# Six feed-forward chunks as seven block products per two chunks, weight sums on GpSimd, attention in two sets of buffers

## The chip, the cores and the metric

The kernel runs on one core of one Trainium2 chip. The metric is the device time of one execution in microseconds (us). Three executions of the kernel before took 1272.78, 1272.90 and 1273.23 us; the median is 1272.9 us. Engines are named as the profile names them: PE (matrix products; PEld is its weight load), DVE (vector), ACT (scalar), POOL (GpSimd), SP (which issues most of the DMAs).

## The reference

Linear attention with random features feeds a gated feed-forward layer. Attention has 8 batches of 8 heads with 576 tokens and 64 columns, so 4608 tokens of 512 columns enter the feed-forward layer, whose hidden width is 1536.

```python
def phi(x):
    proj = einsum('bhsd,df->bhsf', x, w_phi)
    proj = proj - max(abs(proj), axis=-1, keepdims=True)
    return concatenate([exp(proj), exp(-proj)], axis=-1)
q_p, k_p = phi(q), phi(k)
kv = einsum('bhsf,bhsd->bhfd', k_p, v);  z = sum(k_p, axis=2)
num = einsum('bhsf,bhfd->bhsd', q_p, kv)
den = einsum('bhsf,bhf->bhs', q_p, z)[..., None] + 1e-06
x = (num / den).transpose(0, 2, 1, 3).reshape(4608, 512)
g = x @ w_gate;  silu = g * (1.0 / (1.0 + exp(-g)));  val = x @ w_val
return silu * val @ w_out
```

## The kernel before

**Precision.** Most products are built from fp32r operands: a number is split into a high part (ACT rounds it) and a low part (DVE subtracts the high part), and a product is three matmuls: high by high, high by low, low by high. In the trace such an fp32r matmul is one record; a matmul of plain fp32 operands is two records.

**Feed-forward.** The tokens are cut into 12 chunks of 384 (`CH`), the hidden width into 12 strips of 128 (index `f`). `first(c, f, ...)` (L686) computes gate and value of chunk c in strip f: for each of two outputs (banks gv0 and gv1) four blocks of 128 input columns, three matmuls each, so 24 matmuls of 128x384. ACT then takes the tanh (L716) and DVE multiplies twice (L718, L721); `parts` splits the hidden strip into hh (ACT, L741) and hl (DVE, L742). `second(c, f, ...)` (L747) is nine matmuls of 128x512 into the three banks o0 to o2. `put_off` issues the second layer of strip f behind the first layer of strip f+1, so that PE has work while ACT and DVE make the hidden strip. The high parts of the weights stay in SBUF; the low parts are read from DRAM (`low_parts`, L669), anew for each chunk.

**Attention.** `attention(i, rank)` (L341) does one pair of heads, 32 pairs in all, four to a batch. The first eight pairs (`EARLY_PAIRS`) use plain fp32 products and two sets of buffers; the other 24 use one set, and split K, Q, the exponentials of Q (qh and ql, L577 to L583) and the sums kv (kvh and kvl, L456 and L460). The numerators (L593) are products of 128x288: four per pair, each of six fp32r matmuls in a late pair and of two fp32 matmuls in an early one. Behind them DVE divides (L616 to L620), and the result is split into xh and xl (L632, L634), which the first layer reads.

**The order.** Nothing is ordered by hand around the change. Every step is added to a `Plan` with an engine, a cost, the steps that it follows and a rank. `Plan.run` (L88) plays these through and writes out each engine's instructions in a fixed order: the ready step of lowest rank goes first. Attention has its pair number as rank on all engines, feed-forward steps on ACT, DVE and SP have rank -1 (`FIRST`), and feed-forward products on PE have ranks over 1000, so that they fill what attention leaves. Where PE has nothing ready in the plan, it gets products with zeros (L835 to L839), until the last strip of the first chunk.

## Time and profile before

| | |
|---|---|
| three executions | 1272.78, 1272.90, 1273.23 us |
| span of the profiled execution | 1273.1 us |
| instructions | 19796 |
| mean granted PE clock | 0.996 |
| HBM | 131 GB/s over the span |

The span runs from the first to the last instruction of one core; it lies 0.2 us over the median of the three times, so span and time are used alike below. Busy time is the union of an engine's instructions. PE records of neighbouring matmuls overlap (an fp32r matmul of 128x384 is shown with some 335 ns), so what a matmul costs PE is read from the distance of the starts, or from the chain of waits, where a row merges neighbours.

### The profile page before, as it was taken

What the parts mean: (1) busy time and instruction counts of PE and PEld (TensorE: products, weight loads), DVE (VectorE), ACT (ScalarE), POOL (GpSimd) and SP (SyncE); (2) the same over time, 40 slices, a digit from 0 to 9 for tenths busy, and PEclk for the clock granted to TensorE, in tenths of its full rate; (3) what the DMA queues carried; (4) which work ended last, traced back from release to release, by engine and by line L of the source; (5) the groups of instructions that cost most, each with busy time, mean ns of one, the idle gap of its engine ahead of it and who ended that gap; (6) DMA issues with size and microseconds to landing.
All of it is one profiled execution on the core that took longest, in us unless ns stands there. A gap on an engine that the chain in (4) does not pass through costs nothing.

```text
span 1273.1 us, 19796 instructions
## 1 busy us (share of the span) xinstructions
PE 1262.2 (99%) x7427; PEld 1189.9 (93%) x7427; DVE 876.4 (69%) x1674; ACT 651.5 (51%) x1383; POOL 1.3 (0%) x13
## 2 busy tenths in 40 slices
PE   9999999999999999999999999999999999999998
PEld 8887999999889999999999999999999999999998
DVE  6998999998887778762788888822488886222222
ACT  5787433336676666632765666611466665121211
POOL 0000000000000000000000000000000000000000
PEclk8999999999999999999999999999999999999999
DMA  4543455555564344444433444354444342444443
GB/s 120 144 119 102 140 174 175 174 165 167 159 204 123 112 117 113 148 123 127 129 104 113 129 124 120 105 161 129 125 120 119 105 132 84 124 149 125 149 126 106
DMA packets 112111, 168.15 MB, mean 132 GB/s; under 512 B 52752, under 2 KB 59408, under 8 KB 112016
## 3 DMA queue, kind: packets, MB, share of 16 engines
q1 hardware_dynamic: 111552, 166.64, 44.1%
q8 instruction: 58, 0.95, 0.3%
q14 instruction: 37, 0.30, 0.1%
q10 hardware_dynamic: 464, 0.26, 0.1%
HBM read 143.26 MB, written 23.59 MB: 131 GB/s over the span
## 4 chain that ended last, share of the span: by engine, by line
PE 92%; DVE 4%; DMA 1%; ACT 1%; SPq 1%; issue 0%; DVEq 0%; ACTq 0%
PE gv L282 46%; PE o L282 25%; PE work L282 12%; PE kv L435 8%; PE kv L428 1%; DMA out_dram<-osb 0%; PE o L502 0%; DVE km L410 0%; DVE kp L415 0%; DMA shared<-in_wg_dram 0%; DMA shared<-in_wo_dram 0%; DVE qy L491 0%; DMA wbd<-in_w_phi_dram 0%; DVE km L486 0%; ACT den L609 0%
## 5 line engine op out<-in xcount | busy, mean ns | idle before, releaser
L282 PE MATMUL gv<-xh,w_hi 128*128 128x384 f32 x1152 | 388.6, 337 | 0.8 <-DVE th L718 0.8
L282 PE MATMUL gv<-xh,w_lo 128*128 128x384 f32 x1152 | 386.9, 336 | 0.0
L282 PE MATMUL gv<-xl,w_hi 128*128 128x384 f32 x1152 | 386.1, 335 | 0.0
L282 PEld LDWEIGHTS gv<-xh,w_hi 128*128 128x128 f32 x1152 | 216.4, 188 | 5.7 <-DVE th L718 1.1
L282 PEld LDWEIGHTS gv<-xl,w_hi 128*128 128x128 f32 x1152 | 216.5, 188 | 4.6
L282 PEld LDWEIGHTS gv<-xh,w_lo 128*128 128x128 f32 x1152 | 216.1, 188 | 0.0
L716 ACT ACTIVATE th<-gv 128x384 f32<-128x384 f32 x144 | 70.9, 492 | 263.9 <-PE gv L282 263.1
L718 DVE SCALAR_TENSOR_TENSOR th<-th,gv 128x384 f32<-128x384 f32 x144 | 79.2, 550 | 149.6 <-ACT th L716 147.7
L282 PE MATMUL o<-w_hi,hl 128*128 128x512 f32 x432 | 171.5, 397 | 0.2 <-DVE hl L742 0.2
L282 PE MATMUL o<-w_hi,hh 128*128 128x512 f32 x432 | 170.9, 396 | 0.3 <-ACT osb L782 0.3
L282 PE MATMUL o<-w_lo,hh 128*128 128x512 f32 x432 | 170.3, 394 | 0.0
L741 ACT CAST hh<-th 128x384 fp32r<-128x384 f32 x144 | 73.6, 511 | 164.3 <-DVE th L721 148.1
L721 DVE TENSOR_TENSOR th<-th,gv 128x384 f32<-128x384 f32 x144 | 79.4, 552 | 71.1 <-PE gv L282 68.7
L435 PEld LDWEIGHTS kv<-vf,kp 128*128 128x128 f32 x1024 | 123.2, 194 | 3.1 <-ACT kp L419 1.3
L435 PE MATMUL kv<-vf,kp 128*128 128x66 f32 x1024 | 123.2, 274 | 1.3 <-ACT kp L419 1.0
L742 DVE TENSOR_TENSOR hl<-th,hh 128x384 fp32r<-128x384 f32 x144 | 79.5, 552 | 32.8 <-ACT hh L741 32.1
L282 PEld LDWEIGHTS o<-w_hi,hl 128*128 128x128 f32 x432 | 81.4, 188 | 19.4 <-DVE hl L742 0.6
L282 PEld LDWEIGHTS o<-w_hi,hh 128*128 128x128 f32 x432 | 81.7, 189 | 12.7 <-ACT osb L782 0.8
L282 PEld LDWEIGHTS o<-w_lo,hh 128*128 128x128 f32 x432 | 81.4, 188 | 12.2
L616 DVE STREAM_TRANSPOSE qe<-den 128x576 f32<-128x576 f32 x32 | 24.9, 778 | 92.0 <-ACT den L609 92.0
L607 ACT COPY num<-work 64x288 f32<-64x288 f32 x102 | 40.2, 394 | 51.2 <-PE work L282 49.8
L282 PE MATMUL work<-qh,kvh 128*128 128x288 f32 x192 | 60.8, 317 | 0.3 <-DVE kp L415 0.3
(124 smaller groups left out, 1871.1 us busy)
## 6 DMA issues: line engine op xcount, KB each, us to landing
w_lo<-wlo_dram SPq DMA_DIRECT2D x108, 512.0 KB, 3.6
w_lo<-wlo_dram SPq DMA_DIRECT2D x132, 256.0 KB, 3.0
wlo_dram<-w_lo SPq DMA_DIRECT2D x36, 256.0 KB, 2.3
out_dram<-osb SPq DMA_DIRECT2D x35, 256.0 KB, 3.3
kin<-in_kT_dram SPq DMA_DIRECT2D x32, 256.0 KB, 2.9
vf<-in_v_dram SPq DMA_DIRECT2D x64, 128.0 KB, 2.7
qin<-in_qT_dram SPq DMA_DIRECT2D x24, 288.0 KB, 2.9
shared<-in_wg_dram SPq DMA_DIRECT2D x12, 512.0 KB, 3.6
```

Source lines behind the costliest of these rows:

```text
L282: nc.tensor.matmul(o, l, r, start=a, stop=z)
L428: nc.tensor.matmul(ps_kv[:, 2 * k * D2:2 * (k + 1) * D2], room[:, 0, k], vf[j][:, 4].rearrange("p h d -> p (h d)"), start=False, stop=k == 1)
L435: nc.tensor.matmul(o, room[:, 2 * (t - t0) + h, k], vf[j][:, t, h], start=t + h + k == 0, stop=False)
L607: copied.append(add("ACT", act(SH), lambda key=key, ra=ra, c=c: nc.scalar.copy(num[ra, c], work[plan.bank[key]][ra, :SH]), [nu, free], rank))
L616: t0 = add("DVE", dve(S), lambda: vec.transpose(turned, den), [*copied, *done[0], *done[1]], rank)
L716: s1 = add("ACT", act(CH), lambda: nc.scalar.activation(t_, ps_gv[0][:, :CH], AF.Tanh, scale=0.5), [ends[0], th_free[j]], FIRST)
L718: s2 = add("DVE", dve(CH), lambda: nc.vector.scalar_tensor_tensor(out=t_, in0=t_, scalar=1.0, in1=ps_gv[0][:, :CH], op0=ALU.add, op1=ALU.m ...
L721: s3 = add("DVE", dve(CH), lambda: nc.vector.tensor_tensor(out=t_, in0=t_, in1=ps_gv[1][:, :CH], op=ALU.mult), [s2, ends[1]], FIRST)
L741: s4 = add("ACT", act(CH), lambda: nc.scalar.copy(hh[b], th[j]), [made, hid_free[b]], FIRST)
L742: s5 = add("DVE", dve(CH), lambda: nc.vector.tensor_tensor(out=hl[b], in0=th[j], in1=hh[b], op=ALU.subtract), [s4], FIRST)
```

## The change

The last six chunks are no longer done one by one. They are taken two at a time (chunks 6 and 7, 8 and 9, 10 and 11), and for each strip f the eight block products of {gate, value} by {two halves of the input columns} by {two chunks} are replaced by seven products of sums of blocks (Winograd's form of Strassen's product). One block product is six matmuls of 128x384.

- `operands(c)` loads the four blocks of x of two chunks from DRAM, makes sums and differences of them (DVE, 128x768), and splits the seven operands (ACT and DVE, 128x768), once for two chunks.
- `weights(m)` makes the four sums of weight blocks of a strip on POOL: four additions of high and low part (`whole`) and four subtractions (`combine`), each 128x256; ACT then rounds the 128x1024 result (`g2`) and DVE subtracts for the low part (`g3`). One buffer, b_full, holds the sums, two sets hold the results.
- `pair(c, base, ready)` issues the seven products of a strip (p1, p2, p6, p7, p5, p4, p3, called p by their names in the code) into banks gv0 and gv1, with three copies of gv0 by ACT (`copy`) and three additions by DVE (`joined`) that build the four results, and between them, one by one as `part(n)`, the six parts of the second layer of the strip before, for both chunks, into six banks.
- The low weights of the first layer are read once for two chunks.

All buffers of attention and of the pair stage become views of four big tiles (`m1`, `m2`, `a1`, `a2`), each of which is allocated up to three times in turn. So the names in the order and the trace are these tiles from now on. Attention has two sets of buffers throughout. The numerators of the 24 late pairs are plain fp32 products; the splits of the exponentials and of kv are gone, and so is the split of K of pair 8. All attention is finished before the pair stage begins; results of tokens of chunks 6 to 11 are stored to DRAM (x_dram) and not split there.

Core of the diff:

```diff
+PAIRS = 6
+LOW_SETS = 3
+ROOM = {"m1": 6912, "m2": 5140, "a1": 2432, "a2": 2048}
+URGENT = -0.8
+T_SETS = 2
+LOW2_SETS = 4
...
-    kin, qin = [sb("kin", [P, SK])] * 2, [sb("qin", [P, SK])] * 2
-    vf = [sb("vf", [P, 5, 2, D2])] * 2
-    kp = sb("kp", [P, 2, 2, 2, NF], F32, 2)
-    kvs = sb("kvs", [P, 4 * P], F32, 2)
-    qx, qe = sb("qx", [P, 2, S], F32, 2), sb("qe", [P, 2, S], F32, 2)
-    num, den = sb("num", [P, S]), sb("den", [P, S])
...
+    qx, qe = ([view("m1", [2, S]) for _ in range(2)] for _ in range(2))
+    kp = [view("m1", [2, 2, 2, NF]) for _ in range(2)]
+    kvs = [view("m2", [4 * P]) for _ in range(2)]
+    qy = [view("m2", [4, NF]) for _ in range(2)]
+    kin, qin = [view("m2", [SK])] * 2, [view("m2", [SK])] * 2
+    vf = [view("m2", [5, 2, D2])] * 2
+    num, den = view("m2", [S]), view("m2", [S])
...
-        split = not early
-        j = i % 2 if early else 1
+        plain = i <= EARLY_PAIRS
+        j = i % 2
+        one = 0 if early else j
...
-        if split:
-            for ones in range(2):
-                kvc.append(add("DVE", dve(4 * D), lambda ones=ones: vec.tensor_tensor(
-                    out=cut(kv_low(), ones), in0=sums(ones), in1=cut(kv_high(), ones), op=ALU.subtract),
...
-        done = [[f1], [f1]]
-        if split:
-            done = [[], []]
-            for h in range(2):
-                for k in range(2):
-                    part = (qe, qx)[k][j]
-                    def rounded(k=k, h=h, part=part):
-                        take_over()
-                        nc.scalar.copy(qh[k][:, h], part[:, h])
-                    g0 = add("ACT", act(S), rounded, [(f0, f1)[k][h], last.get(("nu", i - 1)), *weights_done], rank)
-                    done[h] += [g0, add("DVE", dve(S), lambda k=k, h=h, part=part: vec.tensor_tensor(
-                        out=ql[k][:, h], in0=part[:, h], in1=qh[k][:, h], op=ALU.subtract), [g0, f1[h]], rank)]
...
+        done = [[f1], [f1]] if early else [[f1[h]] for h in range(2)]
...
-                        if split:
-                            kvh, kvl = kv_high(), kv_low()
-                            terms += [(kvh[:, n], qh[k][:, h, c]), (kvl[:, n], qh[k][:, h, c]), (kvh[:, n], ql[k][:, h, c])]
-                        else:
-                            terms.append((kvs[j][:, n], (qe, qx)[k][j][:, h, c]))
+                        terms.append((kvs[j][:, n], (qe, qx)[k][j][:, h, c]))
...
-                nu = add("PE", 6 * pe(SH) if split else 2 * pe32(SH), numerators, [*done[h], *kvc, nu], rank, take=key)
-                free = last.get(("num", i - 1))
+                nu = add("PE", 2 * pe32(SH), numerators, [*done[h], *kvc, nu], rank, take=key)
...
+        held = [(start, width) for c, at, start, width in cuts if c >= PAIRS]
+        if held:
+            start, width = held[0][0], sum(w for _, w in held)
+            token = b * S + start - PAIRS * CH
+            x_stored[b, pr] = add("SP", P * width * 4, lambda start=start, width=width, token=token: nc.sync.dma_start(
+                x_dram[pr, :, token:token + width], num[:, start:start + width]), [t3], rank)
+            last["num", i].append(x_stored[b, pr])
...
+    attend(PAIRS * CH)
+    spread = []
+    for c in range(EARLY, PAIRS):
+        if c == PAIRS - 1:
+            attend(NCH * CH)
...
+        def whole():
+            for n in range(4):
+                gp.tensor_tensor(out=full()[:, block(n)], in0=hi[:, block(n)], in1=get(low)[:, block(n)], op=ALU.add)
+        def combine():
+            x = full()
+            for o, l, r in ((0, 2, 0), (2, 3, 2), (3, 3, 0), (1, 1, 3)):
+                gp.tensor_tensor(out=x[:, block(o)], in0=x[:, block(l)], in1=x[:, block(r)], op=ALU.subtract)
+        g0 = add("POOL", 4 * pool2(2 * P), whole, [low_at[m], *b_free], NEXT)
+        g1 = add("POOL", 4 * pool2(2 * P), combine, [g0], NEXT)
+        g2 = add("ACT", act(8 * P), lambda: nc.scalar.copy(th_(), full()), [g1, *t_free[u]], NEXT)
+        g3 = add("DVE", dve(8 * P), lambda: nc.vector.tensor_tensor(out=t(), in0=full(), in1=th_(), op=ALU.subtract), [g2], NEXT)
+        b_free[:] = [g3]
+        lo_free[k].append(g0)
+        t_free[u] = []
+        t_at[m] = [g2, g3]
...
+        d1 = combine(s1, a21, a22, ALU.add, [got[2], got[3], *temp_free[4]])
+        d2 = combine(s2, s1, a11, ALU.subtract, [d1, got[0], *temp_free[5]])
+        d3 = combine(a21, a11, a21, ALU.subtract, [d1, got[0]])
+        l0 = split(0, a11, [got[0]])
+        l1 = split(1, a12, [got[1]])
+        l2 = split(2, s2, [d2])
+        l3 = split(3, a21, [d3])
+        l4 = split(4, s1, [d1])
+        l5 = split(5, a22, [got[3]])
+        d4 = combine(a12, a12, s2, ALU.subtract, [l1, d2])
+        l6 = split(6, a12, [d4])
...
+            def mult(j, o, begin, final, after, m=m, low=low, hi=hi, tl=tl, t_hi=t_hi):
+                if j in (0, 1, 6):
+                    at = block((0, 1, None, None, None, None, 3)[j])
+                    w = lambda: (hi[:, at], get(low)[:, at])
+                    made = [low_at[m]]
+                    free = lo_free[m % LOW_SETS]
+                else:
+                    at = block((3, 2, 0, 1)[j - 2])
+                    w = lambda: (t_hi()[:, at], tl()[:, at])
+                    made = t_at[m]
+                    free = t_free[m % T_SETS]
...
+                    w_hi, w_lo = (x.rearrange("p (k f) -> p k f", k=2) for x in w())
+                    a_hi, a_lo = get(op_hi[j]), get(op_lo[j])
+                    terms = [x for k in range(2) for x in (
+                        (w_hi[:, k], a_hi[:, k]), (w_hi[:, k], a_lo[:, k]), (w_lo[:, k], a_hi[:, k]))]
+                    for i, (l, r) in enumerate(terms):
+                        nc.tensor.matmul(o[:, :CH], l, r, start=begin and i == 0, stop=i == len(terms) - 1, skip_group_check=True)
...
+            def copy(n, after):
+                return add("ACT", act(CH), lambda: act_.copy(snap[n](), bank_b[:, :CH]), [after, *snap_free[n]], FIRST)
+            def joined(n, after):
+                return add("DVE", dve(CH), lambda: vec.tensor_tensor(
+                    out=snap[n](), in0=bank_c[:, :CH], in1=snap[n](), op=ALU.add), after, FIRST)
...
+            p1 = mult(0, bank_b, True, False, b_read)
+            y1 = copy(0, p1)
+            p2 = mult(1, bank_c, True, True, c_read)
+            g1 = joined(0, [p2, y1])
+            ja, ga = gate(snap[0], [g1])
+            p6 = mult(2, bank_b, False, False, [y1])
+            y2 = copy(1, p6)
+            part(0)
+            part(1)
+            p7 = mult(3, bank_b, False, False, [y2])
+            y3 = copy(2, p7)
+            part(2)
+            p5 = mult(4, bank_c, True, False, [g1])
+            v2 = joined(2, [p5, y3])
+            p4 = mult(5, bank_b, False, True, [y3])
+            jb, gb = gate(bank_b[:, :CH], [p4])
+            part(3)
+            p3 = mult(6, bank_c, False, True, [v2])
+            v1 = joined(1, [p3, y2])
+            part(4)
+            part(5)
+            b_read[:], c_read[:] = [gb], [v1]
+            hb = valued(jb, 2, [gb, v2])
+            side_b = parts(jb, hb)
+            ha = valued(ja, 1, [ga, v1])
+            side_a = parts(ja, ha)
+            snap_free[:] = [[ga], [ha], [hb]]
+            waiting.append((c, f, side_a, side_b, low2(m), (outs, last_half) if final else None))
...
+    weights(0)
+    weights(1)
+    for n in range((NCH - PAIRS) // 2):
+        pair(PAIRS + 2 * n, NFT * n, operands(PAIRS + 2 * n))
+    at, g, ha_, hb_, lo2, tail = waiting.pop()
+    second(at + 1, g, hb_, lo2, range(NT), NT, tail)
+    second(at, g, ha_, lo2, range(NT), 0, tail)
```

What moves on the engines is seen in their order at three places. The first is PE, in the first layer of a late chunk: of before, the end of the value sum of chunk 10, where xh_98 and xl_101 are the chunk's parts, w_hi_76 and w_lo_94 the strip's weights, and the rows that follow are the second layer of the strip before.

```order
L282 MATMUL gv_144<-xh_98,w_hi_76 128x384
L282 MATMUL gv_144<-xl_101,w_hi_76 128x384
L282 MATMUL gv_144<-xh_98,w_lo_94 128x384
L282 MATMUL o_140<-w_hi_87,hh_130 128x512
L282 MATMUL o_140<-w_lo_95,hh_130 128x512
L282 MATMUL o_140<-w_hi_87,hl_132 128x512
```

Now, in the last pair of chunks: a part of the second layer (work_133), then the product p5 (into gv_130) and the start of p4 (into gv_129), whose weights are the sums in m_2_6847.

```order
L312 MATMUL work_133<-w_hi_84,hh_118 128x512
L312 MATMUL work_133<-m_2_6847,hh_118 128x512
L312 MATMUL work_133<-w_hi_84,hl_120 128x512
L1006 MATMUL gv_130<-a_2_6959,m_2_6847 128x384 x6
L1006 MATMUL gv_129<-xh_100,m_2_6847 128x384
L1006 MATMUL gv_129<-xl_103,m_2_6847 128x384
L1006 MATMUL gv_129<-xh_100,m_2_6847 128x384 x2
```

Of matmuls of 128x384 with operands the whole program has 3456 before and 3240 now; those of 128x512 stay at 1296. A strip of two chunks is now 42 and 18 of them in turn, with parts of the second layer between the products, instead of 48 and 18.

The second place is PE, in the numerators of a late pair. Before, with the exponentials' parts qh and ql and the sums' parts kvh and kvl:

```order
L282 MATMUL work0_146<-qh0_2562,kvh_1212 128x288
L282 MATMUL work0_146<-qh0_2562,kvl_1229 128x288
L282 MATMUL work0_146<-ql0_2563,kvh_1212 128x288
L282 MATMUL work0_146<-qh1_2564,kvh_1212 128x288
L282 MATMUL work0_146<-qh1_2564,kvl_1229 128x288
L282 MATMUL work0_146<-ql1_2565,kvh_1212 128x288
```

Now, for the last pair, where m1_0_104 holds the exponentials and m2_0_105 the sums, with a piece of a first layer between two numerators:

```order
L312 MATMUL work1_133<-m1_0_104,m2_0_105 128x288 x2
L312 MATMUL work0_132<-m1_0_104,m2_0_105 128x288 x2
L312 MATMUL gv1_130<-xh2_100,w1_hi7_77 128x384
L312 MATMUL gv1_130<-xl2_103,w1_hi7_77 128x384
L312 MATMUL gv1_130<-xh2_100,w1_lo1_95 128x384
```

Each of the 96 late numerators is two fp32 matmuls where it was six fp32r ones. The last of them stands 145 rows ahead of the first block product.

The third place is ACT in a late strip. Before, it does a tanh and a cast per strip:

```order
L716 ACTIVATE th_127<-gv_143 128x384
L741 CAST hh_131<-th_127 128x384
L716 ACTIVATE th_128<-gv_143 128x384
L741 CAST hh_130<-th_128 128x384
L716 ACTIVATE th_129<-gv_143 128x384
```

Now one strip of two chunks, where L1014 copies the bank gv0, L1024 is the tanh of the one and the other chunk, L922 the cast of the weight sums that POOL made (it waits for POOL), and L765 the casts of the two hidden strips:

```order
L1014 COPY m_2_6850<-gv_129 128x384 [waits PE_49,Activation_49]
L1024 ACTIVATE th_114<-m_2_6850 128x384 [waits DVE_49]
L1014 COPY a_2_6891<-gv_129 128x384 [waits PE_49] x2
L1024 ACTIVATE th_115<-gv_129 128x384 [waits PE_49]
L922 CAST m_2_6847<-a_2_6891 128x1024 [waits Pool_49]
L765 CAST hh_118<-th_115 128x384 [waits DVE_49]
```

ACT executes in this order; behind the cast that waits for POOL stand the casts of the hidden strips and the first copy of the next strip.

More of the change, by code (lines that the diff above doesn't have):

```diff
@@ L59 @@
 class Plan:
-    LAG = {"PE": 220, "ACT": 90, "DVE": 90, "SP": 2000}
+    LAG = {"PE": 220, "ACT": 90, "DVE": 90, "POOL": 200, "SP": 2000}
     BYTES = 250.0
@@ L135, in start @@
                 n += 1
-                heapq.heappush(events, (freed if t.eng == e and e in ("ACT", "DVE", "PE") else done, n, "dep", t))
+                heapq.heappush(events, (freed if t.eng == e and e in ("ACT", "DVE", "PE", "POOL") else done, n, "dep", t))
             if s.give is not None:
@@ new lines, in attention, with clear @@
+        use = lambda name: [last.get((name, i - 2)), last.get((name + "'", i - 2))]
+        if i == EARLY_PAIRS + 1:
+            def clear():
+                nc.gpsimd.memset(vf[1]()[:, :, :, D:], 1.0)
+                for h in range(2):
+                    nc.gpsimd.memset(vf[1]()[h * D:(h + 1) * D, 4, 1 - h], 0.0)
+                    nc.gpsimd.memset(kin[1]()[h * D:(h + 1) * D, 4 * P + (1 - h) * D:4 * P + (2 - h) * D], 0.0)
+            last["vf", i - 2] = last["kin", i - 2] = last["qin", i - 2] = add("POOL", 1000, clear, weights_done, rank)
@@ L363, in attention @@
         else:
-            q_in = [add("SP", P * S * 4, lambda: nc.sync.dma_start(qin[j][:, :S], qT[b, pr]), [last.get(("qin", i - 1))], rank)]
+            q_in = [add("SP", P * S * 4, lambda: nc.sync.dma_start(get(qin[one])[:, :S], qT[b, pr]), before("qin"), rank)]
         n = 4 * P * P
@@ L399, in project @@
                     acc = o[:, :NF] if tail else o[:, (t - t0) * 256:(t - t0 + 1) * 256]
-                    if early:
-                        matmuls([(acc, kin[j][:, c], wst if tail else wbd, True, True)])
+                    if plain:
+                        matmuls([(acc, get(kin[one])[:, c], wst if tail else wbd, True, True)])
                     else:
-                        khi, klo = (k_parts()[:, n, c] for n in range(2))
+                        khi, klo = (ks()[:, n, c] for n in range(2))
                         w_hi, w_lo = (wst_hi, wst_lo) if tail else (wbd_hi, wbd_lo)
@@ L440, in attention @@
         last["khi", i] = kproj
-        if early:
+        if plain:
             last["kin", i] = kproj
@@ L621, in attention @@
         last["qe", i] = t1
-        last["qx", i], last["qx'", i] = (done[0][-1], done[1][-1]) if split else (nu, None)
+        last["qx", i], last["qx'", i] = nu, None
         odd = b % 2
@@ L792, in favor_attention_moe @@
+            u = osb[n % len(osb)] if tail is None else tail[0][base + t]
+            cp = add("ACT", act(DM), lambda o=o, u=u: nc.scalar.activation(get(u), o, AF.Copy, scale=0.5),
+                     [done, out_done.get(n - len(osb)) if tail is None else None], FIRST)
+            stored[base + t] = [cp]
+            out_done[n] = add("SP", P * DM * 4, lambda u=u, rows=rows: nc.sync.dma_start(rows(), get(u)), [cp], FIRST)
     made = [0]
@@ new lines, in favor_attention_moe, with weights @@
+    b_free = list(ended)
+    t_free = [list(ended) for _ in range(T_SETS)]
+    for k in range(NT, 2 * NT):
+        stored[k] = list(ended)
+    low_at, t_at = {}, {}
+    def weights(m):
+        f = m % NFT
+        gp = nc.gpsimd
+        k, u = m % LOW_SETS, m % T_SETS
+        low, hi, t, th_, full = lo_bufs[k], flat(w1_hi[f]), t_low[u], t_high[u], b_full
+        after, lo_free[k] = lo_free[k], []
+        low_at[m] = add("SP", P * 8 * P * 4, lambda: nc.sync.dma_start(get(low).bitcast(F32), wlo_dram[f, :, :2 * DM]),
+                        [lo_stored[f, 0], lo_stored[f, 1], *after], NEXT)
+        def whole():
[13 more added lines that the diff above has]
+        t_at[m] = [g2, g3]
```

298 lines of the change are left out of this document (208 added, 90 removed).

## The prediction

> **What bounds the kernel now.** I read the busy times first, then the slices, the windows, the chain of waits and, for prices, single engines in order of time. The page begins:
>
> ```profile
> PE 1262.2 (99%) x7427; PEld 1189.9 (93%) x7427; DVE 876.4 (69%) x1674; ACT 651.5 (51%) x1383; POOL 1.3 (0%) x13
> ...
> DVE  6998999998887778762788888822488886222222
> ...
> PEclk8999999999999999999999999999999999999999
> ...
> PE 92%; DVE 4%; DMA 1%; ACT 1%; SPq 1%; issue 0%; DVEq 0%; ACTq 0%
> PE gv L282 46%; PE o L282 25%; PE work L282 12%; PE kv L435 8%; PE kv L428 1%; DMA out_dram<-osb 0%; PE o L502 0%; DVE km L410 0%; DVE kp L415 0%; DMA shared<-in_wg_dram 0%; DMA shared<-in_wo_dram 0%; DVE qy L491 0%; DMA wbd<-in_w_phi_dram 0%; DVE km L486 0%; ACT den L609 0%
> ```
>
> PE is busy in all slices, at full clock, and it carries 92% of the chain that ended last; first-layer products (gv) alone are 46%. A busy PE could still be a slow one, so I look where it waits. Windows (span, then busy us of PE, PEld, DVE, ACT and POOL with counts, clock, DMA share, GB/s):
>
> ```profile
> 0.00:300.00 300.00, 294.07 (x1717) 276.25 (x1718) 270.84 (x522) 164.89 (x349) 1.34 (x13) 0.99 0.47 145
> 300.00:1100.00 800.00, 799.03 (x4830) 756.26 (x4829) 560.21 (x1072) 455.11 (x972) 0.00 (x0) 1.00 0.44 128
> 1100.00:1273.00 173.00, 169.12 (x885) 157.35 (x883) 45.32 (x82) 31.53 (x62) 0.00 (x0) 1.00 0.43 130
> ```
>
> PE idles 6 us in the first 300 us, 1 us in the next 800, and at the end for little more than the last copy and store. So **PE's own instructions are the time**, and an instruction less on PE is worth its whole distance to the next. The attention work keeps DVE at 70% between 300 and 1100 us; after that DVE and ACT are nearly free.
>
> **The change, term by term.** The chain gives the price of a feed-forward matmul (start, us, what):
>
> ```profile
> 890.39 4.19 PE gv L282 x24
> 896.67 4.19 PE gv L282 x24
> 902.95 4.19 PE gv L282 x24
> ```
>
> 24 matmuls of 128x384 take 4.19 us, 0.1746 us each; the strips start 6.28 us apart, so the nine of the second layer take 2.09 us. The order of the changed kernel has 3240 of the former where there were 3456: 216 x 0.1746 = **37.7 us less**. Two chunks' strip costs PE 42 x 0.1746 + 2 x 2.09 = 11.51 us instead of 12.56; there are 36 of these, 414 us in all.
>
> Against it stand the late numerators. PE in order of time, first four fp32 numerators of an early pair, then one fp32r numerator of a late one:
>
> ```profile
> 64.33 0.65 PE L282 MATMUL o<-qe,kvs 128*128 128x288 f32 x2
> ...
> 67.73 0.65 PE L282 MATMUL o<-qx,kvs 128*128 128x288 f32 x2
> 68.22 1.90 PE L435 MATMUL kv<-vf,kp 128*128 128x66 f32 x16
> ```
>
> ```profile
> 626.37 0.30 PE L282 MATMUL work<-qh,kvh 128*128 128x288 f32 x1
> ...
> 627.04 0.29 PE L282 MATMUL work<-ql,kvh 128*128 128x288 f32 x1
> 627.17 1.89 PE L435 MATMUL kv<-vf,kp 128*128 128x66 f32 x16
> ```
>
> The eight fp32 matmuls last from 64.33 to 68.22, 3.89 us, so 0.97 us a numerator; the six fp32r ones last 0.80 us. 24 pairs of four numerators: 96 x 0.17 = **16.3 us more**. The K of pair 8 goes from five projections in fp32r to fp32; if they become dearer in the same ratio, 1.7 us become 2.1, which I leave in the range. The second layer's 1296 matmuls stay. Net on PE: -37.7 + 16.3 = **-21.4 us**; 1273.1 - 21.4 = 1251.7 us, if PE waits no more than now.
>
> **Do DVE and ACT still keep up?** First the attention stage. All 32 pairs must now be done ahead of the last 414 us, so in about 1252 - 414 = 838 us. What leaves DVE, and what is laid on it (mean ns):
>
> ```profile
> L582 DVE TENSOR_TENSOR ql<-qx,qh 128x576 fp32r<-128x576 f32 x48 | 36.2, 754 | 0.0
> L460 DVE TENSOR_TENSOR kvl<-kv,kvh 128x256 fp32r<-128x256 f32 x48 | 18.7, 417 | 0.0
> L742 DVE TENSOR_TENSOR hl<-th,hh 128x384 fp32r<-128x384 f32 x144 | 79.5, 552 | 32.8 <-ACT hh L741 32.1
> L380 DVE TENSOR_TENSOR ks<-kin,ks 128x640 fp32r<-128x640 f32 x24 | 19.7, 822 | 4.7 <-ACT ks L378 3.8 <-DMA qin<-in_qT_dram 0.7
> L378 ACT CAST ks<-kin 128x640 fp32r<-128x640 f32 x24 | 17.2, 715 | 0.1
> L741 ACT CAST hh<-th 128x384 fp32r<-128x384 f32 x144 | 73.6, 511 | 164.3 <-DVE th L721 148.1 <-PE o L282 13.9 <-DVE qe L559 1.6
> ```
>
> Four low parts of exponentials and two of kv per late pair: 24 x (4 x 0.754 + 2 x 0.417) = 92 us off DVE. The feed-forward work of six chunks, 72 strips of three DVE operations of 0.55 us, is 119 us. So DVE has about 876 - 92 - 119 = 665 us in 838: 79% (a little less, as the late x is no longer split there). The first 300 us, at 271 us of DVE, held the weights too; of what follows, 394 us fall into 538, or 73%. That is near the 70% at which PE waited 1 us in 800, and there are two sets of buffers where there was one. The new stores of x keep one buffer, num, until they land:
>
> ```profile
> out_dram<-osb SPq DMA_DIRECT2D x35, 256.0 KB, 3.3
> ```
>
> A store of like size takes 3.3 us, and the next pair's numerators come some 20 us later (538 / 24 is 22), so the wait of ACT's copies for it costs nothing; SP's queue meanwhile loses half of the low-weight loads of six chunks. I take no new wait, and keep as upper end what the first 300 us show at 90% of DVE: 6 us of wait in 300, so 11 in 538.
>
> Then a strip of two chunks, 11.5 us of PE. DVE does nine operations of 128x384 (three additions, three in the gates and three more behind them are 0.55 us each by the row of hl), and the low part of the weight sums, 128x1024: by the rows at 384 and 640 columns, 0.270 us per 256, that is 1.23 us. Sum 6.2 us. ACT does seven of 0.5 us and a cast of 128x1024, 1.02 us by its two rows: 4.5 us. Both fit, so what counts is order and latency. These rows, from one window, give the latency:
>
> ```profile
> 1142.95 0.33 PE L282 MATMUL gv<-xh,w_lo 128*128 128x384 f32 x1
> 1143.32 0.49 ACT L716 ACTIVATE th<-gv 128x384 f32<-128x384 f32 x1 [3.04 <-PE gv L282]
> 1143.85 0.55 DVE L718 SCALAR_TENSOR_TENSOR th<-th,gv 128x384 f32<-128x384 f32 x1 [2.98 <-ACT th L716]
> ```
>
> ACT starts 0.37 us after the start of the last matmul, 0.2 us after PE could issue the next; DVE follows ACT by 0.04. Laid against the code of one strip (a product is 1.05 us, a part 0.70): the copy of p1 is done 0.2 + 0.5 us behind it, and p2 covers 1.05. The copy of p6 has two parts, 1.4 us, over it, that of p7 a part and p5. The addition behind p5 has p4 and a part, 1.75 us, over it. The tightest is the addition behind p3: on DVE it stands behind the low part of the weight sums, which ends at 11.3 us of the strip (cast at 9.05, where the second tanh is over, then 1.02, then 1.23), so it ends near 11.85; p2 of the next strip wants its bank at 12.5. That leaves **0.65 us**.
>
> The new engine in this loop is POOL, and the new wait is that of ACT's cast for it. Behind that cast in ACT's queue stand the two casts of the hidden strips and the next strip's first copy, for which DVE and then PE wait. It starts on the next sums when that low part is done, at 0.1 us of the next strip, and is wanted at 9.05: 8.9 us for eight operations of 128x256. The trace has no such operation on POOL; the nearest rows on it are these:
>
> ```profile
> masks.py:199 POOL TENSOR_SCALAR_AFFINE_SELECT ident<-ident 128x128 f32<-128x128 f32 x1 | 0.3, 288 | 0.0
> L267 POOL MEMSET vf<- 128x20 f32 x1 | 0.1, 117 | 0.0
> ```
>
> Taking 0.1 us of it as start, the select costs 1.47 ns a column; 256 columns are 0.1 + 0.38 = 0.48 us if a second operand is free and 0.1 + 0.75 = 0.85 us if it costs as much again. I take 0.65 us, the middle, as both ends scale the same row; bounds 0.48 and 0.85. Eight are 5.2 us, with some 0.5 us for five waits of POOL on itself. The sums are thus ready near 6 us of the strip, 3 us early, and cost PE nothing; at 0.85 us, 7.3 us, still nothing. The Trainium skill (GPSIMD Engine Reference, 3.1 Elementwise) states 4497 ns for an addition of 2048 columns; a column share of that is an estimate of 0.56 us. By it the sum is the same and the slow rival below would lose half its chance; no run shown here has the operation.
>
> At the two changes of pair ACT casts and DVE subtracts seven operands of 128x768 within about a strip, and DVE makes four sums. At 0.27 us per 256 columns each is 0.95 us: 11 us more on DVE over two strips with 12.4 of 23. DVE is then full, and I allow 1 us of wait for each change, 2 in all, and 0.04 us a strip, 1.5 us, for jitter. **Forecast: 1251.7 + 3.5, about 1255 us** of span, and of time, which differ by 0.2 us.
>
> **The rivals.**
>
> *POOL and DVE get in each other's way (0.20).* Of DVE's operations in a strip six read two SBUF operands (the first gate, two products with the value, two low parts of the hidden strip, the low part of the sums). If one such and one on POOL exclude each other, each waits for half to all of a POOL operation, 0.33 to 0.65 us: 2 to 3.9 us on DVE per strip. That still fits 11.5 us, but not always the 0.65 us of slack; at 0.3 us lost per strip it is 36 x 0.3 = 11 us, so 1263 (1259 to 1270). For it: DVE's order in the strip is fixed and full of short dependencies. Against it: the additions that PE waits for read one operand from PSUM. The Trainium skill (SBUF — State Buffer, Who interferes with whom) says that the two engines share a read port as an exclusive lock and that a DVE instruction with two SBUF inputs contends with a POOL one that reads. By that rule this rival happens in kind; the trace of before, with POOL idle beside DVE, cannot show it.
>
> *The attention stage thins out (0.13).* With 20 us or less for a late pair, a pair's chain of DVE and ACT steps decides, and PE runs out of ready products: 6 to 11 us by the rate of the first 300 us, so 1259 to 1266. For it: the rate of those 300 us came with DVE at 90%. Against it: by the order PE has feed-forward rows between all attention rows and 145 rows left after the last numerator.
>
> *POOL is too slow: slower than before (0.10).* POOL has 8.9 us; with 2.2 us lost to four DVE operations of 0.55 us and 0.5 us for its own waits, eight operations must fit 6.2 us, and PE feels it beyond another 0.65 us. A strip loses 0.59 us, all that it gained net (21.4 / 36), at 8.9 + 0.65 + 0.59 = 10.1 us of POOL time: **from 0.93 us an operation on, the change loses**. At 1.0 us it is (10.7 - 9.55) x 36 = 41 us, so 1293. 0.93 lies above my upper bound of 0.85, and every 0.1 us costs 29 us.
>
> That the change doesn't do what it says is excluded by the order: the 216 matmuls are gone, the 96 numerators are there.
>
> **How the numbers follow.** The forecast holds with 0.57, from 1248 (no new wait, and 3 us of today's wait gone) to 1260. Both middle rivals end below 1270. So 1248 to 1270 holds some 0.85, with the slow rival and what lies under 1248 left out. A measurement of this kernel tells differences over 0.2%, 2.5 us. Faster by more: 0.57 + 0.19 + 0.11 = 0.87; within: 0.03; slower: 0.10.
>
> **What would show it.** In the profile after: PE 99% busy in all slices; the chain with gv near 1273 x 46% - 38 = 548 us; a numerator of two fp32 matmuls at 0.97 us; strips of two chunks 11.5 us apart; POOL some 5 to 6 us busy per strip and never the last to be waited for by ACT. PE waits on ACT's copies or on DVE's additions at 11.5 us spacing would prove the lock; ACT waits at the cast for POOL the slow POOL; PE idle between 300 and 800 us the thin attention. I am wrong if a POOL operation takes over 0.9 us, or if PE's price of a product changes when weights and operands are new tiles.

## The result, and the profile after

| | before | after |
|---|---|---|
| median of four executions | 1272.84 us | 1262.76 us |
| lowest to highest | 1271.03 to 1273.23 | 1262.39 to 1264.82 |
| span of the profiled execution | 1273.1 us | 1260.7 us |

The ratio is 0.9933, with a 95% interval of 0.9916 to 0.995: the change makes the kernel 0.7% faster. The forecast had been 1255 us, 1.4% faster. The direction holds, and so does the wide range (1248 to 1270), but not the narrower one, up to 1260, in which the forecast was to hold: some 10 us of the 18 came, and nearly half of the gain is missing.

The page of the changed kernel, busy time (us, share of the span, instructions), slices, and the chain of waits by engine and line:

```profile
span 1260.7 us, 19274 instructions
PE 1241.0 (98%) x7008; PEld 1145.7 (91%) x7008; DVE 943.2 (75%) x1674; ACT 688.3 (55%) x1419; POOL 246.9 (20%) x306
...
PE   9999999999999999999999999989999999999998
...
POOL 0000000000000000000000000285565665565550
...
PE 90%; DVE 4%; POOL 2%; DMA 1%; ACT 1%; issue 1%; SPq 0%; DVEq 0%; POOLq 0%
PE gv L312 23%; PE gv L1006 19%; PE o L312 19%; PE work L312 17%; PE kv L472 8%; PE kv L312 2%; PE kv L465 1%; POOL a L913 1%; POOL a L918 1%; DMA a<-in_wg_dram 1%; DVE m L951 0%; PE o L534 0%; DVE xl L955 0%; DMA m<-wlo_dram 0%; DVE km L447 0%
```

PE's busy time falls from 1262.2 to 1241.0 us, by 21.2; the forecast was 21.4. So PE's part is as worked out, and the missing gain is idle time of PE: 1260.7 - 1241.0 = 19.7 us against 10.9 before. Ahead of the last slice one slice of PE has an 8, just where POOL's work begins, and POOL appears in the chain with 2%. Windows show where PE idles (span, then busy us of PE, PEld, DVE, ACT and POOL with counts, clock, DMA share, GB/s):

```profile
0.00:300.00 300.00, 294.55 (x1708) 275.64 (x1709) 265.82 (x513) 162.37 (x343) 1.93 (x18) 1.00 0.48 152
...
300.00:800.00 500.00, 500.00 (x3006) 457.49 (x3005) 394.86 (x756) 340.38 (x739) 0.00 (x0) 1.00 0.41 124
800.00:850.00 50.00, 43.77 (x221) 40.06 (x220) 36.48 (x42) 18.93 (x32) 31.92 (x31) 0.97 0.55 191
850.00:900.00 50.00, 50.00 (x262) 46.48 (x261) 29.05 (x45) 19.26 (x35) 26.79 (x34) 1.00 0.21 65
900.00:1000.00 100.00, 97.87 (x501) 90.19 (x500) 68.54 (x97) 43.88 (x80) 56.97 (x66) 0.98 0.31 102
1000.00:1100.00 100.00, 100.00 (x521) 93.08 (x520) 55.98 (x85) 37.40 (x70) 56.12 (x71) 1.00 0.20 64
1100.00:1200.00 100.00, 98.35 (x513) 91.35 (x513) 64.62 (x95) 44.43 (x81) 57.33 (x68) 1.00 0.26 87
1200.00:1260.70 60.70, 56.42 (x289) 51.40 (x287) 27.81 (x47) 21.61 (x41) 15.80 (x21) 0.99 0.15 53
```

Attention's stage from 300 to 800 us has no idle time at all. In the pair stage PE loses 6.2 us at the start of the first pair of chunks (800 to 850), 2.1 and 1.65 at the starts of the second and third, and nothing in between: with POOL at 56 us of 100, a strip of two chunks runs without a wait (521 matmuls in 100 us, 60 to a strip, so 11.5 us each). The first 300 us and the end cost 5.5 and 4.3 us, as before.

What PE waits for in the pair stage (us in total, times, longest):

```profile
PE gv L1006 <- DVE a L1017: 4.9, 3, 1.8
PE gv L1006 <- DVE th L742: 2.5, 1, 2.5
PE gv L1006 <- ACT m L1014: 2.5, 2, 2.1
```

It waits for DVE first of all, 7.4 of 9.9 us. So I looked at what DVE does at the first start, in order of time (start, us, instruction, idle time before it):

```profile
822.14 1.50 DVE L955 TENSOR_TENSOR a<-m,a 128x768 fp32r<-128x768 f32 x1
823.56 2.89 DVE L955 TENSOR_TENSOR xl<-m,xh 128x768 fp32r<-128x768 f32 x2
826.37 0.54 DVE L742 SCALAR_TENSOR_TENSOR th<-th,gv 128x384 f32<-128x384 f32 x1
...
833.99 4.32 DVE L951 TENSOR_TENSOR m<-m 128x768 f32<-128x768 f32 x3
838.23 0.54 DVE L1017 TENSOR_TENSOR a<-gv,a 128x384 f32<-128x384 f32 x1
```

and at PE's three rows behind its waits at this start:

```profile
826.97 0.69 PE L1006 MATMUL gv<-xh,w_hi 128*128 128x384 f32 x1 [2.53 <-DVE th L742]
...
838.83 0.44 PE L1006 MATMUL gv<-xh,w_hi 128*128 128x384 f32 x1 [1.52 <-DVE a L1017]
...
844.34 0.44 PE L1006 MATMUL gv<-xh,m 128*128 128x384 f32 x1 [2.09 <-ACT m L1014]
```

The gate of the chunk before (L742) frees the bank that the first product wants. It takes 0.54 us itself, but stands in DVE's queue behind splits of the operands (L955) at 1.45 us each. The second wait is of the same kind: three sums of operands (L951), 1.44 us each, ahead of an addition (L1017) that lasts 0.54 us. The step in the prediction had 0.95 us for such an operation. The third wait goes through ACT and POOL. The copy that PE waits for (L1014, at 843.81 us) stands in ACT's queue behind a cast that waits for POOL:

```profile
842.45 1.04 ACT L922 CAST m<-a 128x1024 fp32r<-128x1024 f32 x1 [1.90 <-POOL a L918]
```

POOL had spent 8.7 us (833.68 to 842.42) on the eight operations behind this cast. What it does ahead of that, beside DVE's work:

```profile
808.66 2.82 POOL L913 TENSOR_TENSOR a<-w_hi,m 128x256 f32<-128x256 f32 x4 [525.20 <-DMA m<-wlo_dram]
811.43 4.70 POOL L918 TENSOR_TENSOR a<-a 128x256 f32<-128x256 f32 x4
819.86 5.78 POOL L913 TENSOR_TENSOR a<-w_hi,w_lo 128x256 f32<-128x256 f32 x4 [3.73 <-DVE m L951]
825.60 5.66 POOL L918 TENSOR_TENSOR a<-a 128x256 f32<-128x256 f32 x4
```

Its four additions take 2.82 us in the first row and 5.78 us in the third, beside those splits: both engines are longer when they run together. The groups of DVE by shape (count, busy us, mean ns, idle before) set the two kinds of operand against each other:

```profile
L1025 DVE SCALAR_TENSOR_TENSOR th<-th,m 128x384 f32<-128x384 f32 x36 | 34.1, 947 | 3.6 <-ACT th L1024 3.2
...
L955 DVE TENSOR_TENSOR xl<-m,xh 128x768 fp32r<-128x768 f32 x18 | 22.9, 1291 | 0.0
...
L1025 DVE SCALAR_TENSOR_TENSOR th<-th,gv 128x384 f32<-128x384 f32 x36 | 19.9, 552 | 29.7 <-ACT th L1024 29.7
L951 DVE TENSOR_TENSOR m<-m 128x768 f32<-128x768 f32 x12 | 14.9, 1263 | 0.1
```

L1025 is one instruction in two uses. With one operand in PSUM (gv) it takes 552 ns; with both in SBUF (th and m) it takes 947.

### The profile page after: what moved, and what is told of

It reads as the page before. It is cut to its first block, busy times and chain, and to the rows that moved or that the text cites. A ratio compares the mean times of both kernels' runs of the same rounds, so it can differ in the third digit from the quotient of the medians.

```text
span 1260.7 us, 19274 instructions
## 1 busy us (share of the span) xinstructions
PE 1241.0 (98%) x7008; PEld 1145.7 (91%) x7008; DVE 943.2 (75%) x1674; ACT 688.3 (55%) x1419; POOL 246.9 (20%) x306
## 4 chain that ended last, share of the span: by engine, by line
PE 90%; DVE 4%; POOL 2%; DMA 1%; ACT 1%; issue 1%; SPq 0%; DVEq 0%; POOLq 0%
PE gv L312 23%; PE gv L1006 19%; PE o L312 19%; PE work L312 17%; PE kv L472 8%; PE kv L312 2%; PE kv L465 1%; POOL a L913 1%; POOL a L918 1%; DMA a<-in_wg_dram 1%; DVE m L951 0%; PE o L534 0%; DVE xl L955 0%; DMA m<-wlo_dram 0%; DVE km L447 0%
## 5 line engine op out<-in xcount | busy, mean ns | idle before, releaser
L312 PE MATMUL gv<-xh,w_hi 128*128 128x384 f32 x576 | 201.6, 350 | 1.4 <-DVE th L742 1.4
L312 PE MATMUL gv<-xl,w_hi 128*128 128x384 f32 x576 | 193.2, 335 | 0.0
L312 PE MATMUL gv<-xh,w_lo 128*128 128x384 f32 x576 | 193.2, 335 | 0.0
L1006 PE MATMUL gv<-xh,m 128*128 128x384 f32 x504 | 151.3, 338 | 2.6 <-ACT m L1014 2.5
L918 POOL TENSOR_TENSOR a<-a 128x256 f32<-128x256 f32 x144 | 117.5, 816 | 8.5
L312 PEld LDWEIGHTS gv<-xh,w_hi 128*128 128x128 f32 x576 | 108.3, 188 | 5.1 <-DVE th L742 2.0
L312 PEld LDWEIGHTS gv<-xl,w_hi 128*128 128x128 f32 x576 | 108.3, 188 | 3.2 <-DVE xl L657 0.2
L1017 DVE TENSOR_TENSOR a<-gv,a 128x384 f32<-128x384 f32 x72 | 39.9, 553 | 94.4 <-PE gv L1006 94.2
L312 PE MATMUL work<-m,m 128*128 128x288 f32 x408 | 109.4, 406 | 0.0
L312 PEld LDWEIGHTS gv<-xh,w_lo 128*128 128x128 f32 x576 | 108.1, 188 | 0.0
L1006 PEld LDWEIGHTS gv<-xh,m 128*128 128x128 f32 x504 | 93.7, 189 | 5.7 <-ACT m L1014 3.3
L1006 PE MATMUL gv<-xh,w_hi 128*128 128x384 f32 x216 | 73.7, 341 | 7.5 <-DVE a L1017 4.9
L765 ACT CAST hh<-th 128x384 fp32r<-128x384 f32 x108 | 55.3, 512 | 44.0 <-DVE th L745 30.6
L1006 PE MATMUL gv<-xl,w_hi 128*128 128x384 f32 x216 | 73.4, 340 | 0.0
```

What stands on the lines that cost most here:

```text
L312: nc.tensor.matmul(o, l, r, start=a, stop=z)
L765: s4 = add("ACT", act(CH), lambda: nc.scalar.copy(get(hh[b]), th[j]), [made, hid_free[b]], FIRST)
L918: gp.tensor_tensor(out=x[:, block(o)], in0=x[:, block(l)], in1=x[:, block(r)], op=ALU.subtract)
L1006: nc.tensor.matmul(o[:, :CH], l, r, start=begin and i == 0, stop=i == len(terms) - 1, skip_group_check=True)
L1017: return add("DVE", dve(CH), lambda: vec.tensor_tensor(out=snap[n](), in0=bank_c[:, :CH], in1=snap[n](), op=ALU.add), after, FIRST)
```

## The experiments

**Theory A:** POOL's reading of SBUF holds up DVE's instructions with two SBUF operands, and the lengthened block of operand work at the starts of pairs makes PE wait. **Rivals:** B, POOL's sums come late, and PE waits for them through ACT's cast; C, attention ends later than its PE work allows; D, the products or numerators are mispriced.

**e1: the sums are made for the first strip only.**

```diff
-        g0 = add("POOL", 4 * pool2(2 * P), whole, [low_at[m], *b_free], NEXT)
-        g1 = add("POOL", 4 * pool2(2 * P), combine, [g0], NEXT)
+        if m == 0:
+            g0 = add("POOL", 4 * pool2(2 * P), whole, [low_at[m], *b_free], NEXT)
+            g1 = add("POOL", 4 * pool2(2 * P), combine, [g0], NEXT)
+        else:
+            g0, g1 = low_at[m], b_free[0]
```

> Leaves out the weight sums on GpSimd (POOL) of all strips but the first; casts, low parts and products stay, so PE, ACT and DVE have the same instructions. Theory A (the changed kernel's PE waits of some 10 us at the starts of the three pairs of chunks come from POOL and DVE holding each other up): operand splits on DVE fall from 1.29 to about 0.95 us, PE idle between 800 us and the end falls by 7 to 9 us, time 1254 to 1256 us. Theory B (DVE is simply full there, or attention ends too late, POOL is bystander): splits stay, PE idle falls by under 2 us, time 1261 to 1263 us.

Measured: 1253.24 us, ratio 0.9853 (0.9837 to 0.9868). The same groups and the first window of the pair stage in this kernel:

```profile
L1028 DVE SCALAR_TENSOR_TENSOR th<-th,m 128x384 f32<-128x384 f32 x36 | 20.1, 558 | 7.5 <-ACT th L1027 4.3
...
L958 DVE TENSOR_TENSOR xl<-m,xh 128x768 fp32r<-128x768 f32 x18 | 17.7, 1004 | 0.0
L954 DVE TENSOR_TENSOR m<-m 128x768 f32<-128x768 f32 x12 | 11.2, 951 | 1.3 <-DMA m<-x_dram 1.2
```

```profile
800.00:850.00 50.00, 48.54 (x250) 44.02 (x249) 35.89 (x52) 23.18 (x40) 7.25 (x8) 1.00 0.59 201
```

DVE's durations are back at 0.56 and 0.95 us, PE idles 1.5 us where it idled 6.2, and the ratio is that of the forecast (1255 / 1272.9 = 0.986). So the missing gain hangs on POOL's work; C and D are not needed for it. But this takes away POOL's reads, POOL's lateness and its place in the queues at once.

**e6: POOL writes but does not read.** Eight memsets of 128x1024 in a strip, chosen to take about as long.

```diff
-                gp.tensor_tensor(out=full()[:, block(n)], in0=hi[:, block(n)], in1=get(low)[:, block(n)], op=ALU.add)
+                gp.memset(full(), 0.5 + n)
...
-                gp.tensor_tensor(out=x[:, block(o)], in0=x[:, block(l)], in1=x[:, block(r)], op=ALU.subtract)
+                gp.memset(x, 0.25 * (n + 1))
```

> Leaves out the sums: in their place POOL writes constants into the same buffer (eight writes of 128x1024, some 7 us a strip as before), so POOL is as busy but reads nothing from SBUF. If the hold-up is at reading: DVE's splits at 768 columns take 0.95 us as without POOL, time 1253 to 1255 us. If any work of POOL holds DVE up (writing, or both): splits stay near 1.3 us and time near 1261 to 1264 us.

Measured: 1257.64 us, ratio 0.9901 (0.9883 to 0.992).

```profile
L913 POOL MEMSET a<- 128x1024 f32 x144 | 137.6, 955 | 653.4 <-DVE a L553 489.9 <-DVE m L923 157.3
```

```profile
L1025 DVE SCALAR_TENSOR_TENSOR th<-th,m 128x384 f32<-128x384 f32 x36 | 20.1, 557 | 7.5 <-ACT th L1024 4.3
...
L955 DVE TENSOR_TENSOR xl<-m,xh 128x768 fp32r<-128x768 f32 x18 | 16.8, 950 | 0.6 <-ACT xh L954 0.6
```

```profile
PE gv L1006 <- ACT m L1014: 4.5, 3, 2.4
PE gv L1006 <- DVE a L1017: 1.2, 2, 0.6
```

POOL is as busy as ever (8 x 0.955 = 7.6 us a strip, against 6.8), and DVE is as fast as without it. It is POOL's reading that holds DVE up. The time comes down part of the way only, not to the 1253 to 1255 us of the forecast but by some 3 to 4 us by the ratios, at the edge of what the intervals can tell: PE now waits for ACT's copies, which stand behind the cast that waits for POOL (9.9 us in 7 waits). So lateness (B) has a price too where POOL needs 7.6 us.

**e11: POOL reads, and nobody waits for it.** Eight additions a strip into a spare buffer.

```diff
+    spare = view("a2", [2 * P], F32, 2)
...
+        def idle():
+            for n in range(8):
+                gp.tensor_tensor(out=spare(), in0=hi[:, block(n % 4)], in1=get(low)[:, block(n % 4)], op=ALU.add)
...
+            g0, g1 = add("POOL", 8 * pool2(2 * P), idle, [low_at[m], *b_free], NEXT), b_free[0]
```

> Leaves out the sums of all strips but the first; POOL makes eight additions of 128x256 a strip from the same weights into a spare buffer that nobody reads, so DVE is held up as before but nobody waits for POOL. If holding DVE up is the larger part of the loss: splits near 1.3 us, time 1259 to 1262 us, nearer to the changed kernel than to 1253. If ACT's wait for late sums is the larger part: time 1253 to 1257 us.

Measured: 1261.51 us, ratio 0.9934 (0.9918 to 0.9951).

```profile
L1033 DVE SCALAR_TENSOR_TENSOR th<-th,m 128x384 f32<-128x384 f32 x36 | 37.1, 1031 | 3.0 <-ACT th L1032 3.0
L963 DVE TENSOR_TENSOR xl<-m,xh 128x768 fp32r<-128x768 f32 x18 | 22.7, 1277 | 0.0
```

```profile
PE gv L1014 <- DVE a L1025: 4.2, 3, 1.7
PE gv L1014 <- DVE th L742: 2.6, 1, 2.6
```

The same lengths, the same two waits for DVE, and the same time as the changed kernel. PE's waits for ACT's copies shrink from 2.5 us to 0.4, and one of 0.9 us for a low part on DVE has come. From 800 to 1200 us PE idles 8.3 us here, and 8.5 in the profile of e12. So holding DVE up is enough for a loss of this size when nobody waits for POOL; this is for A. B is not refuted: in the changed kernel 2.1 of the 9.9 us come through the cast that waits for POOL. The two prices do not add up: over e1, e6 loses some 6 us by the ratios and e11 some 10, and the changed kernel, with both, loses no more than e11.

**e12: the changed kernel once more**, beside e11 on the same chip.

> The changed kernel as it is, timed beside the others of this call: 1261 to 1264 us, ratio to the kernel before 0.992 to 0.995.

Measured: 1260.74 us, ratio 0.9926 (0.9911 to 0.9941).

**e4: p3 issued twice in each strip**, for the price of a block product.

```diff
+                    if j == 6:
+                        terms = terms + terms
...
-                s = product(6 * pe(CH), go,
+                s = product((12 if j == 6 else 6) * pe(CH), go,
```

> Issues the seventh product (p3) of every strip twice, so that a strip has eight products again; the sum is then wrong by that product. Theory of the price (PE alone sets the pair stage, a product is 1.05 us): 36 x 1.05 = 37.7 us more, less what the longer strip hides of the waits, time 1292 to 1300 us. Rival (the pair stage is set by POOL, DVE and ACT in turn, PE has room): 15 us more or less, time under 1280 us.

Measured: 1301.22 us, ratio 1.0225 (1.0207 to 1.0244); 38.5 us over the changed kernel's 1262.76 (37.2 by the two ratios), and 38.6 us more of PE's busy time (1279.6). The time lies just above the forecast's 1300 us, and the term of 37.7 us stands.

**e8: half the numerators.** The second of the two matmuls of each of the 96 late numerators is left out.

```diff
-                        terms.append((kvs[j][:, n], (qe, qx)[k][j][:, h, c]))
+                        if early or k == 0:
+                            terms.append((kvs[j][:, n], (qe, qx)[k][j][:, h, c]))
...
-                nu = add("PE", 2 * pe32(SH), numerators,
+                nu = add("PE", (2 if early else 1) * pe32(SH), numerators,
```

> Leaves out the second of the two matmuls of each of the 96 late numerators. If PE alone sets the attention stage and an fp32 matmul of 128x288 costs 0.485 us: 96 x 0.485 = 46.6 us less, time 1214 to 1219 us, and the price of the numerators' change (16.3 us) stands. Rival (DVE at 80% sets the pace of attention): PE waits appear between 300 and 800 us and less than 35 us is gained, time 1228 us or more.

Measured: 1256.63 us, ratio 0.9895 (0.9873 to 0.9916).

```profile
300.00:800.00 500.00, 482.78 (x2939) 445.08 (x2938) 401.63 (x768) 345.40 (x746) 0.00 (x0) 0.98 0.44 132
800.00:850.00 50.00, 30.74 (x122) 27.01 (x123) 33.27 (x36) 18.11 (x29) 32.93 (x32) 0.69 0.39 124
```

```profile
PE gv L1007 <- ACT xh L955: 18.5, 2, 10.3
PE work L312 <- ACT m L596: 9.3, 2, 7.5
```

The forecast of 46.6 us less failed, and the rival came true. PE's busy time falls by 38.4 us (to 1202.6), the time by 4 to 5 (by the ratios): PE now idles 17.2 us in attention's stage and 19.3 behind it. Attention hardly ends earlier (its last store of x is issued by 798 us, in the changed kernel at 800.8), as its own steps on DVE and ACT set its end. PE is busy throughout in the changed kernel because feed-forward work just suffices to fill it. The 38.4 us are no price of a numerator either, as the granted clock was 0.69 in the second window. The price stands by the changed kernel's own trace: the eight records of two late numerators start 0.24 us apart (603.72 to 605.41 us), which makes 0.97 us each, as forecast. So the numerators' 16.3 us are busy time of PE, but to make them cheaper would win little here.

**Three ways round the holding up.** e2 makes the sums of the first three strips on DVE, e3 gives the plan a POOL cost near the measured one (1.0 us for an operation), and e7 does both and adds 0.45 us to the plan's cost of each 128x768 operation on DVE.

```diff
 e2, e7
-        gp = nc.gpsimd
+        on_dve = m < 3
+        gp = nc.vector if on_dve else nc.gpsimd
 e3, e7
-    return 80 + 2.55 * n
+    return 80 + 3.6 * n
```

> Same work, but the weight sums of the first three strips are made on DVE (eight operations of 128x256 at some 0.42 us). Theory A: no mutual hold-up while the first operands are split; of the 6.2 us of PE idle between 800 and 850 us half or more goes, time 1258 to 1260 us. Theory B (DVE full): DVE gets 10 us more work in that stretch and PE waits 3 us or more longer, time 1265 us or more.

> Same work, only the plan's cost of a POOL sum is raised from 0.73 to 1.0 us, near the 0.82 to 0.95 us measured, so that steps behind a sum are put later in the queues. Theory C (the waits come from queue positions that rest on a POOL cost set too low): PE idle after 800 us falls by 2 us or more, time 1260 us or less. Theory A (the hold-up itself): within 1 us of the changed kernel, 1262 to 1264 us.

> Same work: sums of the first three strips on DVE, the plan's cost of a POOL sum 1.0 us, and of an operand sum or split on DVE 0.45 us more, near what they take beside POOL. Theory (hold-up remains, but the order no longer rests on prices without it): PE idle after 800 us under 9 us, time 1256 to 1259 us, better than either of the two single changes (1261.5 and 1260.2). Rival (the hold-up moves the waits elsewhere): 1260 us or more.

Measured: 1261.52 us, 0.9913 (0.9898 to 0.9929); 1260.21 us, 0.9906 (0.9891 to 0.9922); and 1263.12 us, 0.9944 (0.9928 to 0.996). e2 and e7 miss the times that theory A forecast, and e3 falls between those of its two theories. None can be told from the changed kernel, whose two ratios are 0.9933 and 0.9926. In e2 the first start costs PE 2.4 us in place of 6.2, but the strips behind it lose 1.9 us between 850 and 900, and the later starts stay as they were. In e7 PE waits for other instructions (DVE's splits 3.5 us, ACT's casts of the operands 2.4 us). Moving the collision moves the wait.

**e5: all sums on DVE** (on_dve = True).

> Same work, all weight sums on DVE (eight operations of 128x256 a strip), POOL idle. Mutual hold-up: DVE's operations with two SBUF operands keep their price of the kernel before (0.55 us at 384 columns, some 0.95 us at 768), DVE has 6.2 + 3.3 = 9.5 us in a strip of 11.5 us; PE idle after 800 us falls from 14 to 6 to 9 us, time 1255 to 1260 us. Rival (DVE full is what PE waits for): more waits than in the changed kernel, time 1266 us or more.

Measured: 1279.96 us, ratio 1.0078 (1.006 to 1.0097). The time is no price of this layout. In the order that the plan makes here, the cast of the next sums but one comes ahead of p4 in 22 strips, so that p4 reads the sums of another strip there, and PE waits for that cast (21.4 us in 22 waits). Only the durations count:

```profile
L919 DVE TENSOR_TENSOR a<-a 128x256 f32<-128x256 f32 x144 | 60.9, 423 | 3.7
```

A sum takes DVE 0.42 us, and with POOL idle the splits (L957) are at 949 ns. What all sums on DVE would cost in the right order stays open.

**e9 and e10: fewer sums.** The sums depend on the weights alone, and the changed kernel makes them anew for each pair of chunks. e9 makes them in the first pair, stores both parts to DRAM, and loads them for the other two; it also adds the sums of strip m+2 to the plan behind the products of strip m, and has e3's cost. e10 makes the first two strips' sums on DVE besides.

```diff
+        if m >= NFT:
+            after, t_free[u] = t_free[u], []
+            t_at[m] = [add("SP", P * 8 * P * 4, lambda n=n, x=x: nc.sync.dma_start(get(x).bitcast(F32), t_dram[f, n]),
+                           [*t_stored[f], *after], NEXT) for n, x in enumerate((th_, t))]
+            return
...
-        t_free[u] = []
+        t_free[u] = t_stored[f] = [add("SP", P * 8 * P * 4, lambda n=n, x=x: nc.sync.dma_start(t_dram[f, n], get(x).bitcast(F32)),
+                                       [g2, g3], NEXT) for n, x in enumerate((th_, t))]
```

> Same products. POOL makes the weight sums only for the first pair of chunks; their high and low parts are stored to DRAM and loaded again for the other two pairs (1 MB a strip), so that POOL, the 128x1024 cast and the 128x1024 low part are gone from 24 of 36 strips; plan's POOL cost 1.0 us; a strip's sums are made behind the products of the strip before last. Theory A (POOL, by holding DVE up and by being waited for, makes the waits): PE idle between 900 and 1200 us falls from 3.8 to under 1 us, time 1256 to 1259 us. Rival (the loads of 1 MB a strip are late, or operand splits alone fill DVE): waits of 3 us or more at the two later starts, 1260 us or more.

> As the one before, and the sums of the first two strips on DVE. Theory A: of the PE idle from 800 to 850 us (6.2 us in the changed kernel) half or more goes: 1254 to 1257 us. Rival: DVE full at that place, no better than the one before.

Measured: 1255.05 us, 0.9879 (0.9861 to 0.9896), and 1254.12 us, 0.9866 (0.9848 to 0.9885). Windows of e10 from the first start on:

```profile
800.00:850.00 50.00, 46.98 (x241) 42.37 (x240) 39.31 (x63) 20.49 (x36) 10.98 (x12) 1.00 0.76 263
...
900.00:1000.00 100.00, 100.00 (x524) 93.25 (x523) 61.27 (x93) 41.73 (x78) 27.80 (x33) 1.00 0.55 196
1000.00:1100.00 100.00, 100.00 (x521) 92.90 (x520) 44.93 (x82) 31.89 (x65) 0.00 (x0) 1.00 0.47 166
1100.00:1200.00 100.00, 100.00 (x523) 93.22 (x522) 48.58 (x87) 35.54 (x71) 0.00 (x0) 1.00 0.49 173
```

Once POOL is done, the start of a pair costs PE nothing: 100.00 in the windows of the second and third. The loads (166 GB/s where there were 64) hide. This is not POOL's part alone: in these 24 strips the cast of the sums (1.05 us of ACT) and their low part (1.22 us of DVE) are gone as well. Neither leaves anything out; e10 is 1.3% faster than the kernel before and beats the changed one too, its interval (to 0.9885) lying under both of that one's (from 0.9911).

## Why the prediction was right in direction and wrong in size

**Right.** *The products*, -37.7 us: 37 to 38.5 by e4. *Net on PE*, -21.4 us: 21.2 by the busy times. *A strip of two chunks* at 11.5 us, with no wait in the middle of a pair, as forecast. *Attention's stage*: "I take no new wait", and its windows show none; e8 adds that it had little to spare. *POOL fast enough*: in the strips PE loses nothing to it, but that was in part luck. 6.8 us a strip lie within the 8.9 us of the prediction, though one operation took 0.82 to 0.95 us on the mean, where 0.65 was taken and 0.85 was the upper bound. Undisturbed it took 0.705 us (2.82 for four). But the 3 us that the prediction had to spare are not there. It let POOL start when the low part is done (at 0.1 us of the next strip, where its own figures, 11.3 of 11.5 us, give 0.2 us before it). In the trace POOL also waits for the load of the low weights, and is done just when ACT comes to the cast:

```profile
925.52 3.46 POOL L913 TENSOR_TENSOR a<-w_hi,w_lo 128x256 f32<-128x256 f32 x4 [4.78 <-DMA w_lo<-wlo_dram]
928.93 3.17 POOL L918 TENSOR_TENSOR a<-a 128x256 f32<-128x256 f32 x4
...
932.14 1.05 ACT L922 CAST m<-a 128x1024 fp32r<-128x1024 f32 x1
```

The low part had ended at 923.1 us here; the tanh ahead of the cast ends at 932.07, the sums at 932.10. And POOL was to be "never the last to be waited for by ACT": the casts wait for it 12.3 us in 13 waits, most of it at the starts of the pairs.

**Wrong: the step on the changes of pair.** "At 0.27 us per 256 columns each is 0.95 us ... I allow 1 us of wait for each change, 2 in all." The duration was scaled from rows of a kernel whose POOL was idle. Beside POOL's reads the operations took 1.26 to 1.29 us on the mean and up to 1.5, and PE waited 6.2 + 2.1 + 1.65 = 10 us at three starts (8.5 in e12's profile of the same kernel); 2.1 of the 10 came through the cast that waits for POOL. Two things were mis-sized. First, the later changes: 3.8 us instead of 2. Second and larger, the first start, from attention to the pairs, has no term at all; the prediction names only the 145 rows of PE work behind the last numerator, and those against another rival. That work lasts to 824.4 us and does cover the load and the first sums, but DVE's queue then holds the operands' work ahead of the gate that frees the bank, and a margin on PE is no margin on DVE.

**The rival that happened** was "POOL and DVE get in each other's way", with a chance of 0.20 and about 1263 us. Its mechanism was right and its place wrong: it looked for 0.3 us lost in every strip against a slack of 0.65. The strips lose nothing: of the six operations with two SBUF operands only the first gate is much longer (0.947 us), while the products with the value and the low parts of the hidden strip stay at 0.58 and 0.62 us in their large groups, and the low part of the sums at 1.22. That the addition behind p3 reads PSUM, and that what stands ahead of it still fits, is argued from its 0.55 us and not tried. The loss comes where DVE is full. That the two sums are alike, 10 us here and 11 there, is chance. The Trainium skill (SBUF — State Buffer, Who interferes with whom) states that DVE's instructions with two SBUF inputs contend with POOL's reading ones for a shared lock; the trace agrees in all three parts: two SBUF operands 0.95 us, one in PSUM 0.55, POOL only writing 0.56. The text weighed that rule, and left its own prices at those of an idle POOL.

**The base.** The forecast took the page's span, 1273.1 us, for a time. In all executions but one the time lies 1.7 to 2.1 us above the span (here 1262.5 over 1260.7), so that page was, by estimate, of an execution of some 1275 us, 2 us over the median. Together: 1255.2 forecast, + 10 - 2 for the starts, - 1.5 for the jitter that did not come, - 1.2 for waits elsewhere (9.7 us now, 10.9 before), + 0.2 on PE's busy time: 1260.7, which is the span; 1.8 more is the time of 1262.5.

**Not tried:** attention's part undone by itself, and the operand work put behind the gates in DVE's order by hand.

## What to carry to other kernels

A duration holds for the neighbours that it was measured with: when a change wakes an idle engine, price the other engine's instructions by operand place, since those with both operands in SBUF became 1.3 to 1.7 times as long here, on the mean. Look for the loss where the slowed engine is already full, here the starts of the pairs, and not in the steady loop. And before tuning where such work runs, ask whether it must run each time: keeping the sums (e10) was worth more than any of the three ways of moving them.
